# Engine orders planned with a later landing for the loads that queue behind the weights, in an attention and feed-forward kernel

## The chip, the cores and the metric

The kernel runs on one core of one Trainium2 chip. The metric is the device time of one execution in microseconds (us), as the median of several executions. A smaller number is better.

A core has five engines with queues of their own: TensorE (PE) for matmuls, VectorE (DVE), ScalarE (ACT), GpSimd (POOL) and SyncE (SP). Each works through its own instructions strictly in the order in which they were written. DMA transfers are issued from queues of SP and POOL.

## The reference

There are two stages. The first is a gated linear attention over 4 batches, 8 heads, 768 steps and a head size of 48:

```python
f = 1.0 / (1.0 + np.exp(-f_logit))
for t in range(S):
    state = f[:, :, t, :, None] * state + np.einsum('bhd,bhe->bhde', k[:, :, t], v[:, :, t])
    y[:, :, t] = np.einsum('bhd,bhde->bhe', q[:, :, t], state)
```

The second takes y as 3072 tokens of 384 features through a feed-forward network with 1536 hidden features:

```python
gate = np.maximum(x @ w_gate, 0.0)
val = x @ w_val
out = gate * val @ w_out
```

Inputs and output are float32; the kernel computes its matmuls in bfloat16.

## The kernel before, in words

**Tiles.** The 768 steps are cut into six chunks c of 128. Within a chunk the batches are taken in pairs pr (b0 = 0 and 2). A load such as q1.0 is q of chunk 1 and pair 0: 384 KB for two batches. For chunks 0 and 1 (twos) two successive chunks are loaded in another layout, and attention_pair works on a pair; from chunk 2 on it is attention_front and attention.

**One pair in attention_pair.** ACT makes exp and ln of f (L583, L584) into bneg. PE sums along the chunk (cum, L592) and ACT takes exponentials of the sums (expo, L606). POOL or DVE multiply k and q with these (hats, L608). PE transposes the hats, first those of k and then those of q, 8 matmuls each for two heads and two chunks (L635), and DVE copies them to qkT (L643). PE forms the scores (L660), DVE masks them into ptm (L669), PE updates the state (L678) and then makes the output rows in the intra block (L698 and L703), which ACT copies to xT (L715).

**The feed-forward part.** It runs one group of 512 tokens per chunk. ffn_hidden makes the gate and val products (L908, 3 matmuls each), ACT takes the relu (L914), and DVE the product gT (L918). ffn_out multiplies with wo (L951), ACT copies to osb (L961), and SP stores it (L965). Its matmuls carry the lowest priority, and are to fill PE between the attention steps.

**The order.** No order is written by hand. Each operation is added to a Plan with the tiles that it reads and writes, an engine, an assumed duration and a priority. schedule() is a list scheduler: again and again it takes the operation that can start earliest in planned time, and of several that can start at once the one with the lowest priority number. The result is one fixed list for each engine, and the waits on semaphores are derived from it afterwards.

**Planned landings.** The loads in the list first are treated more closely:

```python
first = ("f0.0 k0.0 q0.0 v0.0 f0.1 k0.1 q0.1 v0.1 wg0@f0.1 wv0 wg1@q0.1 wv1 wg2 wv2 f1.0@wv1 k1.0 q1.0 v1.0 wo0@q1.0 wo1 wo2 "
         "f1.1 k1.1 q1.1 v1.1").split()
```

The part behind @ is a gate: f1.0 is issued when wv1 has landed, wo0 when q1.0 has landed. The loads f, k, q, v go through SP, the weights wg, wv, wo through POOL. transfers() plays the packets of these two queues against each other. A load of chunk 0 or 1 has 64 packets, of 19 ns each when alone and 27 ns when the two queues alternate; a part of wo has 32 packets, of 62 ns alone and 80 ns in alternation. They begin 2.4 us after the issue (loads) or 2.2 us after it (wo). When the last packet is through, a fixed tail is added and gives the planned landing, Op.land. settle() plans the whole kernel eight times, with the landings of each round as inputs of the next; only the operations in first keep them. Later loads and all stores use a simpler formula in schedule(), which begins where the last of the planned landings ends (flow_free).

So a planned landing has no effect on a transfer by itself. It decides where, on each engine, the operations that depend on a load stand among the others.

Of the kernel before, what the change touches and what calls it, by code (L numbers as in the profile page):

```python
# [5 lines left out]
AF = mybir.ActivationFunctionType  # L6
ALU = mybir.AluOpType
# [35 lines left out]
class Plan:  # L43
# [10 lines left out]
    def add(self, eng, emit, reads=(), writes=(), occ=0.5, lat=0.2, prio=0, opens=(), after=(), follows=()):  # L54
        op = Op(eng, emit, list(reads), list(writes), occ, lat, prio, opens, after, follows)
        op.idx = len(self.ops)
        self.ops.append(op)
        return op
# [128 lines left out]
    def transfers(self):  # L187

        rings = {e: [op for op in self.order[e] if op.parts] for e in ("SP", "POOL")}
        todo, at = {e: [] for e in rings}, {e: 0 for e in rings}  # L190
        issue = {"SP": 0.0}
        held = {e: [] for e in rings}
        sent, owed, t, last = 0, 0, 0.0, None
        pending = None
        sp = rings["SP"]
        queue = {e: [] for e in rings}
        for op in rings["POOL"]:
            queue["POOL"].append([op, op.parts[0], op.start + op.parts[3]])
        nxt = 0

        def feed():
            nonlocal nxt, pending, owed
            while True:
                if pending is not None:
                    if owed - sent > self.depth:
                        return
                    pending.issued = max(t, issue["SP"])
                    issue["SP"] = pending.issued
                    pending = None
                if nxt == len(sp):  # L210
                    return
                op = sp[nxt]
                begin = max(op.ready, issue["SP"])
                if begin > t + 1e-9 and (queue["SP"] or queue["POOL"]):
                    if begin > t + 0.2:
                        return
                nxt += 1
                owed += op.parts[0]
                queue["SP"].append([op, op.parts[0], begin + (op.parts[3] if len(op.parts) > 3 else self.lag)])
                issue["SP"] = begin + op.occ  # L220
                pending = op

        while True:
            feed()
            heads = {e: queue[e][0] for e in queue if queue[e]}
            if not heads:
                break
            can = {e: h for e, h in heads.items() if h[2] <= t}
            if not can:
                times = [h[2] for h in heads.values()]  # L230
                if nxt < len(sp) and pending is None:
                    times.append(max(sp[nxt].ready, issue["SP"]))
                t = max(t + 0.01, min(times))
                continue
            e = next(iter(can)) if len(can) == 1 else ("POOL" if last == "SP" else "SP")
            h = can[e]
            t += h[0].parts[1 if len(can) == 1 else 2] / 1000.0
            last = e
            h[1] -= 1
            if e == "SP":  # L240
                sent += 1
            if h[1] == 0:
                h[0].land = t + (1.6 if e == "POOL" else 0.65 if t < 14.0 else 1.9)
                queue[e].pop(0)

    def settle(self, banks, rounds, early):
        self.depth, self.lag = 250, 2.4
        for i in range(rounds):
            self.schedule(banks)
            if i < rounds - 1:  # L250
                self.transfers()
                for op in self.ops:
                    if op not in early:
                        op.land = op.issued = None
        return self.order
# [47 lines left out]
def bass_hgrn2_outer__then__ffn_reglu_kernel(  # L303
# [8 lines left out]
    out: bass.AP,  # L312
):
    twos = (0, 1)
    pe_hats = set()
    halves = {0: 6, 1: 6, 2: 6}
    x_way = {(c, pr): "tiled" if c < 5 else "xbar" for c in range(6) for pr in range(2)}
    s_twin = {(c, pr) for c in range(6) for pr in range(2)}
# [8 lines left out]
    C = 128  # L327
# [5 lines left out]
    NP = H // 2  # L333
# [14 lines left out]
    hats = sb("hats", [128, NH, 2, H, 64], BF16)  # L348
    NQ = 8
    qkT = sb("qkT", [128, NQ, 2, NP, C], BF16)  # L350
    NM = 4
    ptm_all = sb("ptm", [128, NM, 2, NP, C], BF16)
    ptm = [ptm_all[:, i] for i in range(NM)]
# [34 lines left out]
    add = pl.add  # L388
    gp, ve, sc, te, sy = nc.gpsimd, nc.vector, nc.scalar, nc.tensor, nc.sync
# [7 lines left out]
    def act_t(n):  # L397
        return dict(occ=max(0.18, 0.06 + n / 1150.0), lat=0.14)
# [4 lines left out]
    def pool_t(n):  # L403
        return dict(occ=0.1 + n * 2.2 / 1000.0, lat=0.12)
# [29 lines left out]
    for t, name, src, sname in ((upto, "upto", tri, "tri"), (below, "below", tris, "tris")):  # L434
        add("DVE", lambda t=t, src=src: ve.tensor_tensor(t[:], src[:], same.ap[:, 0:128], ALU.mult), [same, sname], [name],
            occ=0.25, prio=-19)
    add("DVE", lambda: ve.tensor_copy(pick2[:], same.ap[:, 0:128].rearrange("p (b t) -> p b t", b=2)[:, :, 0]), [same], ["pick2"],
        occ=0.1, prio=-19)
    for i, src, name in ((0, upto, "upto"), (1, below, "below"), (1, upto, "upto")):
        lo = [m for m in range(2) if not (i and (name == "upto") != (m == 1))]  # L440
# [3 lines left out]
            prio=-9, **pool_t(64 * len(lo)))  # L444
# [14 lines left out]
    def dma(op, slot, flow, parts, n=1):  # L459

        if slot not in slots:
            slots[slot] = [nc.alloc_semaphore(f"d_{slot}"), 0]
        slots[slot][1] += 16 * n
        op.sem, op.goal = slots[slot]
        op.flow, op.parts = flow, (n * parts[0], *parts[1:])
# [48 lines left out]
    for item in first:  # L514
        item, _, behind = item.partition("@")
        gate = [done[behind]] if behind else []
        if item[0] == "w":
            op = load_w(item[:2], int(item[2:]), gate)
        else:
            c, b = int(item[1]), int(item[3])  # L520
            b0, b1 = (2 * b, 2 * b + 2) if item[2] == "." else (b, b + 1)
            op = load(item[0], c, b0, b1, gate)
# [12 lines left out]
    def hk_(hi):  # L535
        return [f"hk{hi}_0", f"hk{hi}_1"]

    def hq_(hi):
        return [f"hq{hi}_0", f"hq{hi}_1"]

    def qk_(qi):
        return [f"qkT{qi}_{x}{hh}" for x in range(2) for hh in range(2)]

    def tokens(c, b, x, p, lo=0, hi=128, i=None):
        qi = (c * B + b) % NQ
        if c not in twos:
            return qkT[lo:hi, qi, x, p, :]
        row, two = NQ * 2 * NP * C, b % 2
        at = lo * row + (qi - two) * 2 * NP * C + x * 2 * NP * C + p * 2 * C + two * 64
        if i is not None:  # L550
            return bass.AP(tensor=qkT, offset=at + i * C, ap=[[row, hi - lo], [1, 64]])
        return bass.AP(tensor=qkT, offset=at, ap=[[row, hi - lo], [C, 2], [1, 64]])

    t4 = lambda t: t[:, 0:HD].rearrange("p (n j e) -> p n j e", n=NP, j=2)

# [15 lines left out]
    def attention_pair(c, b0):  # L571
        w0 = c * B + b0
        P = w0 * 10
        pr = b0 // 2
# [4 lines left out]
        bi, e0, q0 = (w0 // 2) % NB, w0 % NE, w0 % NQ  # L579
        his = [(w0 + i) % NH for i in range(2)]  # L580
# [6 lines left out]
        for i in range(2):  # L587
# [7 lines left out]
            hi, prod = his[i], {}  # L595
            for x, n in ((1, "k"), (0, "q")):
                e = "DVE" if (i or x if c == 0 else (c, pr, x, i) in on_dve) else "POOL"
# [23 lines left out]
        for j in range(2):  # L621
            lo = 64 * j
# [2 lines left out]
                tot.ap[lo:lo + 64, 0:2 * NP].rearrange("p (n b) -> p n b", n=NP), AF.Exp, scale=-1.0),  # L625
                [tot, "dec0", "dec1"], [f"dec{ai}_{bt}{j}{hh}" for ai in range(2) for hh in range(2)], prio=P + 10,
                follows=[eq_op], **act_t(8))
        for x in (1, 0):
            tp = Bank("tp")

            def transposes(x=x, tp=tp):
                t16 = tp.ap[:, :].bitcast(BF16)
                for p in range(NP):
                    for i in range(2):
                        mm = te.transpose(t16[:, C * (2 * p + i):C * (2 * p + i + 1)],  # L635
                                          hats[:, his[i], x, 2 * p:2 * p + 2, :].rearrange("p h d -> p (h d)"), ident[:])
                return mm
            chain("transposes", "PE", transposes, ["ident"] + [t for hi in his for t in (hk_(hi) if x else hq_(hi))], [tp],
                  occ=0.5, lat=PE_L, prio=P + 4, opens=[tp])
            dst = bass.AP(tensor=qkT, offset=q0 * 2 * NP * C + x * 2 * NP * C, ap=[[NQ * 2 * NP * C, 128], [1, 2 * NP * C]])  # L640
            e = "ACT" if (x, pr) in act_copies else "DVE"
            add(e, (lambda tp=tp, dst=dst: sc.activation(dst, tp.ap[:, :].bitcast(BF16), AF.Copy)) if e == "ACT"
                else (lambda tp=tp, dst=dst: ve.tensor_copy(dst, tp.ap[:, :].bitcast(BF16))),  # L643
                [tp], [f"qkT{q0 + b}_{x}{hh}" for b in range(2) for hh in range(2)], prio=P + 4,
                occ=0.92 if e == "ACT" else 0.61, lat=0.12)

        vs, ms = [(w0 + i) % NV for i in range(2)], [(w0 + i) % NM for i in range(2)]
# [5 lines left out]
        s = [[Bank("s"), Bank("s")] for _ in range(2)]  # L653
# [9 lines left out]
        for its in ((0,), (1,)) if c == 0 else ((0, 1),):  # L663
            at = [t for i in its for t in s[i]]
            chain("scores", "PE", lambda its=its: scores(its), qk, at, occ=0.22 * len(its) + 0.22, lat=PE_L, prio=P + 5, opens=at)
        for i in range(2):
            mask = mask2[:, i, :, :].rearrange("p m t -> p (m t)").unsqueeze(1).to_broadcast([128, NP, C])
            for j in range(2):
                add("DVE", lambda i=i, j=j, mask=mask: ve.tensor_tensor(  # L669
                    ptm[ms[i]][:, j, :, :], s[i][j].ap[:, :].rearrange("p (n t) -> p n t", n=NP), mask, ALU.mult),  # L670
                    [s[i][j], f"mask2_{i}0", f"mask2_{i}1"], [f"ptm{ms[i]}_{j}{hh}" for hh in range(2)], prio=P + 6, **dve_t(512))
# [429 lines left out]
```

## Time and profile before

| | |
|---|---|
| median of 4 runs | 191.53 us |
| lowest and highest | 191.22 and 192.8 us |
| profiled execution, own time | 192.8 us |
| its span, first to last instruction | 191.0 us |
| granted TensorE clock | 1.0 throughout |
| PE busy | 181.7 us (95%) |
| DVE, ACT, POOL busy | 55%, 57%, 39% |
| DMA queues | SP's 28.19 MB, POOL's 3.54 MB |

Busy shares are averages over the span; the loads are read mostly in its first three quarters. PE is pipelined and the ends of its matmuls are modelled, so 95% doesn't say that PE is at its peak. Lines such as L908 are line numbers of the kernel before.

### The profile page before, as it was taken

What the parts mean: (1) busy time and instruction counts of PE and PEld (TensorE: products, weight loads), DVE (VectorE), ACT (ScalarE), POOL (GpSimd) and SP (SyncE); (2) the same over time, 40 slices, a digit from 0 to 9 for tenths busy, and PEclk for the clock granted to TensorE, in tenths of its full rate; (3) what the DMA queues carried; (4) which work ended last, traced back from release to release, by engine and by line L of the source; (5) the groups of instructions that cost most, each with busy time, mean ns of one, the idle gap of its engine ahead of it and who ended that gap; (6) DMA issues with size and microseconds to landing.
All of it is one profiled execution on the core that took longest, in us unless ns stands there. A gap on an engine that the chain in (4) does not pass through costs nothing.

```text
span 191.0 us, 5040 instructions
## 1 busy us (share of the span) xinstructions
PE 181.7 (95%) x2073; PEld 108.9 (57%) x2092; DVE 105.3 (55%) x191; ACT 108.6 (57%) x244; POOL 75.0 (39%) x109
## 2 busy tenths in 40 slices
PE   7978899979999999999999999999999999999995
PEld 2446684546688456768645564554555555544564
DVE  7699766877346867428586274726428323343300
ACT  3763569813889576585877738566533533334322
POOL 8497007861286737536384562908100000000000
PEclk9999999999999999999999999999999999999999
DMA  5999999996999999999999989999531310011113
GB/s 158 325 264 203 207 285 265 221 214 132 250 207 206 223 153 217 225 218 249 168 222 177 225 166 214 180 232 208 127 69 39 86 41 19 23 45 41 41 51 114
DMA packets 108854, 32.04 MB, mean 168 GB/s; under 512 B 101792, under 2 KB 108832, under 8 KB 108832
## 3 DMA queue, kind: packets, MB, share of 16 engines
q1 hardware_dynamic: 104848, 28.19, 69.4%
q0 software_dynamic: 3984, 3.54, 11.7%
q8 instruction: 16, 0.26, 0.6%
q14 instruction: 6, 0.05, 0.1%
HBM read 25.95 MB, written 4.72 MB: 161 GB/s over the span
## 4 chain that ended last, share of the span: by engine, by line
PE 74%; DMA 13%; SPq 7%; POOL 1%; ACT 1%; issue 1%; DVE 0%
PE ps L908 39%; PE ps L951 23%; DMA q_in<-in_q_dram 9%; SPq L486 7%; DMA wv<-in_moe_w_val_dram 5%; PE ps L838 3%; PE ps L803 2%; PE ps L737 1%; PE ps L886 1%; PE ps L931 1%; POOL hats L608 1%; PE ps L698 1%; ACT relu L914 0%; ACT expo L747 0%; PE ps L740 0%
## 5 line engine op out<-in xcount | busy, mean ns | idle before, releaser
L918 DVE TENSOR_TENSOR gT<-relu,ps 128x512 bf16<-128x512 bf16 (+1 forms) x90 | 51.3, 578 | 62.8 <-PE ps L908 36.6
L914 ACT ACTIVATE relu<-ps 128x512 bf16<-128x512 f32 (+1 forms) x90 | 45.8, 513 | 28.5 <-PE ps L908 27.3
L908 PE MATMUL ps<-xT,wv 128*128 128x512 bf16 (+1 forms) x267 | 61.0, 336 | 0.4 <-issue 0.2
L908 PE MATMUL ps<-xT,wg 128*128 128x512 bf16 (+1 forms) x255 | 58.2, 334 | 1.1 <-issue 0.6
L951 PE MATMUL ps<-wo,gT 128*128 128x384 bf16 x276 | 50.0, 326 | 0.0
L908 PEld LDWEIGHTS ps<-xT,wv 128*128 128x128 bf16 x270 | 25.7, 98 | 19.0
L951 PEld LDWEIGHTS ps<-wo,gT 128*128 128x128 bf16 x276 | 26.0, 98 | 17.8
L908 PEld LDWEIGHTS ps<-xT,wg 128*128 128x128 bf16 x270 | 25.1, 98 | 17.6 <-ACT xT L715 0.3
L961 ACT ACTIVATE osb<-ps 128x384 f32<-128x384 f32 x23 | 11.2, 491 | 27.8 <-PE ps L951 27.8
L759 POOL TENSOR_TENSOR hats<-k_in,expo 128x384 bf16<-128x384 f32 x16 | 15.9, 997 | 22.4 <-ACT expo L747 22.4
L813 DVE TENSOR_TENSOR ptm<-ps,tri 128x512 bf16<-128x512 f32 x32 | 20.2, 681 | 2.4 <-PE ps L803 2.4
L568 POOL TENSOR_TENSOR st<-ssum,dec 128x384 bf16<-128x384 f32 x16 | 13.1, 828 | 18.7 <-DVE ssum L566 18.7
L763 POOL TENSOR_TENSOR hats<-q_in,expo 128x384 bf16<-128x384 f32 x16 | 15.7, 998 | 0.5 <-DMA q_in<-in_q_dram 0.5
L566 DVE TENSOR_TENSOR ssum<-ps,st 128x384 f32<-128x384 f32 x16 | 8.7, 553 | 5.6 <-PE ps L886 5.5
L669 DVE TENSOR_TENSOR ptm<-ps,mask 128x512 bf16<-128x512 f32 x16 | 9.9, 681 | 1.1 <-PE ps L660 1.0
L747 ACT ACTIVATE expo<-ps 128x384 f32<-128x384 f32 x16 | 7.9, 492 | 1.8 <-PE ps L740 1.7
L715 ACT ACTIVATE xT<-ps 128x384 bf16<-128x384 f32 x8 | 4.2, 593 | 7.9 <-PE ps L703 7.9
L749 ACT ACTIVATE expo<-ps 128x384 f32<-128x384 f32 x16 | 8.0, 500 | 0.0
L867 ACT ACTIVATE xT<-ps 128x384 bf16<-128x384 f32 x12 | 5.3, 487 | 4.2 <-PE ps L838 4.2
L793 POOL CAST vpad<-v_in 128x384 bf16<-128x384 f32 x16 | 7.6, 505 | 0.0
L730 ACT ACTIVATE bneg<-f_in 128x768 bf16<-128x768 f32 x8 | 6.8, 846 | 0.1
L728 ACT ACTIVATE f_in<-f_in 128x768 f32<-128x768 f32 x8 | 6.7, 842 | 0.0
(83 smaller groups left out, 159.8 us busy)
## 6 DMA issues: line engine op xcount, KB each, us to landing
f_in<-in_f_logit_dram SPq DMA_DIRECT2D x12, 384.0 KB, 5.8
k_in<-in_k_dram SPq DMA_DIRECT2D x12, 384.0 KB, 5.7
q_in<-in_q_dram SPq DMA_DIRECT2D x12, 384.0 KB, 4.9
v_in<-in_v_dram SPq DMA_DIRECT2D x12, 384.0 KB, 5.4
out_dram<-osb SPq DMA_DIRECT2D x23, 192.0 KB, 2.2
wg<-in_moe_w_gate_dram POOLq DMA_DIRECT2D x3, 384.0 KB, 7.8
wv<-in_moe_w_val_dram POOLq DMA_DIRECT2D x3, 384.0 KB, 8.5
wo<-in_moe_w_out_dram POOLq DMA_DIRECT2D x3, 384.0 KB, 8.3
```

The source lines that it names most:

```text
L486: op = add("SP", lambda: sy.dma_start(dst, src), [], in_keys(n, c, b0, b1), occ=0.45 if both else 0.7 if one else 1.0, lat=0.9, prio=c * 1 ...
L566: add("DVE", lambda: ve.tensor_tensor(tmp[:, :], kv.ap[:, 0:HD], s_old[:, :], ALU.add), [kv, f"S{b}_{(c + 1) % 2}"], [key], prio=P + 8, ** ...
L568: add("POOL", lambda: gp.tensor_tensor(t4(s_new), t4(tmp), rate, ALU.mult), [key] + dk, [f"S{b}_{c % 2}"], prio=P + 8, **pool_t(HD))
L669: add("DVE", lambda i=i, j=j, mask=mask: ve.tensor_tensor(ptm[ms[i]][:, j, :, :], s[i][j].ap[:, :].rearrange("p (n t) -> p n t", n=NP), ma ...
L759: add("POOL", lambda: gp.tensor_tensor(hk, kin[:, b % 2, :, :], ex[:, 1, :].rearrange("p (h d) -> p h d", h=H), ALU.mult), in_keys("k", c, ...
L763: add(e, lambda: engine[e].tensor_tensor(hq, qin[:, b % 2, :, :], ex[:, 0, :].rearrange("p (h d) -> p h d", h=H), ALU.mult), in_keys("q", ...
L813: add("DVE", lambda mi=mi, j=j, s=s: ve.tensor_tensor(ptm[mi][:, j, :, :], s.ap[:, :].rearrange("p (n t) -> p n t", n=NP), mask, ALU.mult) ...
L908: mm = te.matmul(bank.ap[:, 0:n], wt[:, kt, j * 128:(j + 1) * 128], xT[xi][:, kt, n0:n1], start=(kt == 0), stop=(kt == NK - 1))
L914: add("ACT", lambda: sc.activation(relu[ri][:, 0:n], gate.ap[:, 0:n], AF.Relu), [gate], [f"relu{ri}"], prio=P, **act_t(n))
L918: add("DVE", lambda: ve.tensor_tensor(gT[gi][:, j, n0:n1], relu[ri][:, 0:n], val.ap[:, 0:n], ALU.mult), [val, f"relu{ri}"], [f"gT{gi}_{j}_ ...
L951: mm = te.matmul(o[b].ap[:, 0:DM], gT[gi][:, j, b * C:(b + 1) * C], wo[:, j, :], start=(j == 0), stop=(j == NJ - 1))
L961: add("ACT", lambda b=b, oi=oi: sc.activation(osb[oi][:, :], o[b].ap[:, 0:DM], AF.Copy), [o[b]], [f"osb{oi}"], prio=P, **act_t(DM))
```

## The change

The number 1.9 in transfers() becomes an entry of a tuple self.tail, which settle() sets to (1.6, 2.6). The 1.6 for POOL's transfers and the 0.65 for SP's landings ahead of 14 us stay as they were.

```diff
-                h[0].land = t + (1.6 if e == "POOL" else 0.65 if t < 14.0 else 1.9)
+                h[0].land = t + (self.tail[0] if e == "POOL" else 0.65 if t < 14.0 else self.tail[1])
...
-        self.depth, self.lag = 250, 2.4
+        self.depth, self.lag, self.tail = 250, 2.4, (1.6, 2.6)
```

The rest of the diff brings switches, and sets them to what the kernel does already: all pairs of chunks 0 and 1 are in pe_hats, so that their hats are transposed on PE with the strides of before, and by_pool is empty.

```diff
-    pe_hats = set()
+    pe_hats = {(0, 0), (0, 1), (1, 0), (1, 1)}
+    by_pool = set()
...
-        at = lo * row + (qi - two) * 2 * NP * C + x * 2 * NP * C + p * 2 * C + two * 64
+        sx, sp, si = (2 * NP * C, 2 * C, C) if (c, b // 2) in pe_hats else (NP * C, C, 2 * NP * C)
+        at = lo * row + (qi - two) * 2 * NP * C + x * sx + p * sp + two * 64
...
+        for i in range(2) if (c, pr) not in pe_hats else ():
+            op = add("SP", lambda i=i: sy.dma_start(qkT[:, q0 + i, :, :, :].rearrange("p x n t -> p (x n) t"),
+                                                    hats[:, his[i], :, :, :].rearrange("p x h d -> p (x h d)"), transpose=True),
...
-        for x in (1, 0):
+        for x in (1, 0) if (c, pr) in pe_hats else ():
...
+                if (c, pr, i, j) in by_pool:
```

More of the change, by code (lines that the diff above doesn't have):

```diff
@@ L548, in tokens @@
         row, two = NQ * 2 * NP * C, b % 2
-        at = lo * row + (qi - two) * 2 * NP * C + x * 2 * NP * C + p * 2 * C + two * 64
+        sx, sp, si = (2 * NP * C, 2 * C, C) if (c, b // 2) in pe_hats else (NP * C, C, 2 * NP * C)
+        at = lo * row + (qi - two) * 2 * NP * C + x * sx + p * sp + two * 64
         if i is not None:
-            return bass.AP(tensor=qkT, offset=at + i * C, ap=[[row, hi - lo], [1, 64]])
-        return bass.AP(tensor=qkT, offset=at, ap=[[row, hi - lo], [C, 2], [1, 64]])
+            return bass.AP(tensor=qkT, offset=at + i * si, ap=[[row, hi - lo], [1, 64]])
+        return bass.AP(tensor=qkT, offset=at, ap=[[row, hi - lo], [si, 2], [1, 64]])
     t4 = lambda t: t[:, 0:HD].rearrange("p (n j e) -> p n j e", n=NP, j=2)
@@ L627, in attention_pair @@
                 follows=[eq_op], **act_t(8))
-        for x in (1, 0):
+        for i in range(2) if (c, pr) not in pe_hats else ():
+            op = add("SP", lambda i=i: sy.dma_start(qkT[:, q0 + i, :, :, :].rearrange("p x n t -> p (x n) t"),
+                                                    hats[:, his[i], :, :, :].rearrange("p x h d -> p (x h d)"), transpose=True),
+                     hk_(his[i]) + hq_(his[i]), qk_(q0 + i), prio=P + 3, occ=1.3, lat=1.2)
+            dma(op, f"qkT{q0 + i}", 1.4, (64, 20, 28))
+        for x in (1, 0) if (c, pr) in pe_hats else ():
             tp = Bank("tp")
@@ L668, in attention_pair @@
             for j in range(2):
+                if (c, pr, i, j) in by_pool:
+                    keys = [f"ptm{ms[i]}_{j}{hh}" for hh in range(2)]
+                    add("ACT", lambda i=i, j=j: sc.activation(ptm[ms[i]][:, j, :, :], s[i][j].ap[:, :].rearrange("p (n t) -> p n t", n=NP),
+                                                              AF.Copy), [s[i][j]], keys, prio=P + 6, **act_t(512))
+                    add("POOL", lambda i=i, j=j, mask=mask: gp.tensor_tensor(ptm[ms[i]][:, j, :, :], ptm[ms[i]][:, j, :, :], mask, ALU.mult),
+                        keys + [f"mask2_{i}0", f"mask2_{i}1"], keys, prio=P + 6, **pool_t(512))
+                    continue
                 add("DVE", lambda i=i, j=j, mask=mask: ve.tensor_tensor(
```

## Prediction

> **What bounds the kernel now.** I began with the chain that ended last, in order of time, then took PE's waits and PE's timeline around the longest of them. Ahead of 43 us the chain is loads, not arithmetic:
>
> ```profile
> 11.76 0.77 POOL wg L507
> 12.53 8.91 DMA wv<-in_moe_w_val_dram
> 21.45 0.37 SPq L486
> ...
> 29.15 11.47 DMA q_in<-in_q_dram
> 40.62 0.07 issue
> 40.69 1.96 POOL hats L608 x2
> 42.64 0.05 issue
> 42.69 0.62 PE ps L635 x8
> ```
>
> Columns: start, duration, what. The loads of chunk 1 start when wv1 has landed; q of its second pair (I write q1.1, its pair 1.1, the first pair 1.0) is issued at 29.15 and lands 11.47 us later, at 40.62; POOL makes two hats; PE transposes them at 42.69. From there the chain is PE almost without a break: no "issue" piece after 43 us is over 0.2 us. So the end is 42.69 plus the PE work still undone then. A gain has to put more PE work ahead of that point.
>
> PE's waits in the whole run say what can be had:
>
> ```profile
> PE ps L1001 <- DVE zeros L414: 1.3, 1, 1.3
> PE ps L635 <- POOL hats L608: 1.1, 1, 1.1
> PE ps L660 <- DVE qkT L643: 1.1, 2, 0.6
> PE ps L908 <- issue: 0.8, 5, 0.2
> ```
>
> Columns: total us, times, longest. The first is the start, and the two of L660 lie at 10.9 and 17.5 us, ahead of any load behind the weights. The second is the one that late landings cause. PE's timeline around it:
>
> ```profile
> 37.68 0.81 PE L908 MATMUL ps<-xT,wg 128*128 128x512 bf16 x3
> 38.42 0.64 PE L660 MATMUL ps<-qkT 48*64 48x128 bf16 x32
> 38.99 0.62 PE L635 MATMUL ps<-ident,hats 128*128 128x128 bf16 x8
> 39.45 0.81 PE L908 MATMUL ps<-xT,wv 128*128 128x512 bf16 x2
> 40.10 1.46 PE L951 MATMUL ps<-wo,gT 128*128 128x384 bf16 x8
> 42.69 0.62 PE L635 MATMUL ps<-ident,hats 128*128 128x128 bf16 x8 [1.13 <-POOL hats L608]
> 43.24 0.74 PE L698 MATMUL ps<-ptm,vpad 64*32 64x128 bf16 x64
> 43.91 0.35 PE L703 MATMUL ps<-qkT,st 128*32 128x128 bf16 x12
> ```
>
> PE stands 1.13 us in front of the q transposes of pair 1.1, and behind them in its queue stands the intra block of pair 1.0 (L698 and L703, 43.24 to 44.2), whose own inputs were ready: its last mask product ended on DVE at 41.67. The order, not the data, keeps it back.
>
> **What the change does, part by part.** All switches but one are neutral: pe_hats holds exactly the pairs that go through attention_pair, so the transposes stay on PE and the strides stay as they were; by_pool is empty. No instruction, DMA or byte is added or removed. Left is the number 1.9 that becomes 2.6: the tail in transfers() between a load's last packet and its planned landing, for SP landings after 14 us. Only the loads of the list first keep these landings, so it concerns the eight loads of chunk 1. The planned times below are the order's inputs, not times of the chip.
>
> (1) The planned landings. By the code the first transfer begins 2.4 us after its planned issue at 21.49 and each takes 64 x 19 ns = 1.216 us, so with 1.9 the landings are 27.00 (f1.0), 28.22, 29.44 (q1.0), 30.65, 31.87, 33.08 (k1.1). The trace (issue plus time to landing) has 26.5, 28.2, 29.2, 31.1, 32.3, 33.4. With 2.6 each moves 0.70 later: the plan gets worse for the first three, better for the next three by little.
>
> q1.1 moves the other way. wo0 is gated on q1.0, and its packets begin 2.2 us after: at 31.64 before, at 32.34 now. q1.1 has the queue from 31.18. Before, 24 of its 64 packets go alone and 40 alternate with wo at 27 + 80 = 107 ns: 31.64 + 4.28 + 1.9 = 37.82. Now 61 go alone and 3 alternate: 32.66 + 2.6 = 35.3. v1.1 likewise goes from 43.96 to about 42.1. In the trace they land at 40.62 and 43.83. So "later landings" holds for six of eight, and the two late ones are planned still earlier.
>
> [...] The row first: 11.47 us from issue to landing for q1.1, and 5.0 to 6.7 for the six ahead of it. [...] By the row, q1.1 shares the DMA engines with wo0 and wo1 and is 2.8 us behind even the old plan: gain up to 1.13. I take the row.
>
> (2) The order on PE, replanned by hand. With f1.0 0.70 later, the bn of pair 1.0 is planned ready at 29.81 instead of 29.34; PE is free at 29.67, so one FFN block (3 matmuls, 0.65 us) goes ahead of the cum matmuls (L592). Everything of pairs 1.0 and 1.1 that hangs on cum moves about 0.65 to 0.8 us later, and one FFN block earlier: no PE work appears or vanishes. On POOL q1.1's landing isn't what binds in either plan: its two hats follow the k hats, and end at 41.29 instead of 40.64. The scores of pair 1.0 now come before an FFN block, so its intra block is ready at about 40.4. When PE is free at 40.69 the intra block is the earliest, and goes **ahead of** the q transposes; before, the transposes went first.
>
> (3) On the chip. The hats cannot end before q1.1's landing plus the 0.07 and 1.96 of the rows, 42.64, in either order. Before, PE ran out at 41.56. Now it has 0.96 us more (43.24 to 44.20) to do there: 1.13 - 0.96 leaves 0.17 of stall, and 0.96 is gained. Against it: on ACT one relu (0.60 in its row) comes ahead of the four exponentials of pair 1.0, which makes the first hats about 0.2 later than PE gets to them; on DVE one gT (0.69) slips between the two q products of that pair (2.35 for both in their row), for another 0.2 to 0.3. Those lie ahead of 42.69, so part of them comes out of the remaining stall: I charge 0.1, with 0 and 0.5 as the bounds. Net gain 0.85, between 0.4 and 1.0.
>
> (4) What moves past the queues. With v1.1 planned 1.9 earlier, the loads of chunk 2 are planned about 1.9 earlier too (f2.0 at 44.4; the trace has 45.4). On SP the load of v2.0 (48.59 now) then comes ahead of the two stores of out (47.54), which wait for ACT: good for the load, and the stores have nobody behind them. POOL keeps its sequence of weight loads; wo2 (issued 34.97) goes 0.7 later but stands behind wo1, which lands at 40.3: free. The cum matmuls of chunk 2 (50.37 now) come 1 to 2 us forward. Their f has landed at 45.4 and needs 0.83 + 0.84 on ACT, so 47.1; I place PE there at 47.5 or later: 0, with 0.5 as the upper bound.
>
> **The sum.** The profiled execution took 192.8 with a span of 191.0; minus 0.85 that is 191.95 and 190.15. It is the highest of the four runs, so I set the 0.85 against the median: 191.53 - 0.85 = 190.7. For gains of 0.4 to 1.2 (the last, should other waits go too): 190.3 to 191.1.
>
> **Rivals.**
> A. The stall stays or moves: intra isn't sorted ahead (a planned 0.6 us decides that), or the waits of pair 1.0 eat it up. For it: the pair's k hats and transposes are already tight (PE waits 0.15 for vpad at 35.08). Against: the margin of 0.6 is most of an FFN block. Time 191.5.
>
> B. Slower. The chunk 2 fronts are ordered by landings that the chip doesn't deliver: f2.1 would be planned at about 53.2 and landed at 55.2 in the trace. With PE about 0.95 behind its plan, ACT would stand 1.05 us in front of that exp, with the relus of the FFN queued behind it; PE has four banks for gate and val and stops after about two more blocks of 0.33. It decides once such waits add to more than 0.85: two pairs at 1.05 each give 191.53 - 0.85 + 2.1 = 192.8; four would give 194.9. For it: the plan is now optimistic where it was about right. Against: PE takes none of its waits there today, ACT is idle 43% of the span, and the issues of these loads move forward as well.
>
> C. More than the stall: PE's other gaps go too. From 54 us PE is busy 133.36 of 137.00, but its waits there are under 1 us together, and nothing in the change is aimed at them. Time 189.5.
>
> **How the numbers follow.** Forecast (190.3 to 191.1) 0.44; A (within 0.4 of 191.5) 0.22; B 0.30, of which half is over 1%; C 0.04. Over 1% (1.9 us, about what a measurement of this kernel can tell from no change): faster 0.04, slower 0.16, within 0.80. The range leaves out C's far end and the quarter or so of B where more than two pairs wait: 189.8 to 193.4.
>
> **What would show it.** Right: in PE's timeline L698 and L703 of pair 1.0 stand ahead of the L635 x8 that follows q1.1, and its wait on hats is under 0.4; q1.1 still lands near 40.6; one more L908 group before the first L592 behind 29 us; v2.0 issued before the first stores. Wrong: the L635 wait at 1 us or more (A); PE waiting on relu, gT or f_in between 50 and 100 us (B); or q1.1 landing elsewhere, which would undo (3).

## The result, and the profile after

| | before | after |
|---|---|---|
| median | 191.85 us (53 runs) | 193.65 us (32 runs) |
| lowest and highest | 191.22 to 195.59 us | 192.33 to 196.24 us |
| profiled execution, own time | 192.80 us | 193.21 us |
| its span | 191.0 us | 191.5 us |

The ratio is 1.0078, with a 95% interval of 1.0061 to 1.0095: the change costs about 1.5 us. That is under 1%, but clearly a loss, where a gain of 0.85 was forecast. Medians are over all executions and ratios over those within 1.5% of the fastest of their kernel, so the two can differ. Line numbers move: L635 is now L642, L698 and L703 are L712 and L717, L592 is L594, L608 is L610, L908 is L922, L951 is L965.

PE's waits in the profile after (total us, times, longest):

```profile
PE ps L717 <- issue: 0.9, 1, 0.9
PE ps L712 <- issue: 0.8, 1, 0.8
PE ps L642 <- POOL hats L610: 0.5, 1, 0.5
```

The wait of 1.1 us in front of the transposes has become one of 0.5. But in the intra block (L712) there is a new stop of 0.85 (0.8 in this view), put down to "issue", that is, to nothing that the profile can name. The stop at L717 lies at 22.45 us; in the profile of before it is there too, with 0.62:

```profile
22.50 0.24 PE L703 MATMUL ps<-qkT,st 128*32 128x128 bf16 x4 [0.62 <-issue]
```

The chain that ended last has the first two one behind the other (start, duration, what):

```profile
28.92 10.00 DMA q_in<-in_q_dram
...
39.06 1.96 POOL hats L610 x2
41.02 0.05 issue
41.06 0.62 PE ps L642 x8
41.68 0.65 PE ps L965 x4
42.34 0.66 PE ps L712 x61
42.99 0.85 issue
43.84 0.21 PE ps L712
```

q1.1 lands at 38.92, 1.7 us earlier than in the profile shown for before, and still PE waits for two hats after it. Which two, and for which transposes, shows in the timelines of POOL and PE:

```profile
37.40 0.99 POOL L610 TENSOR_TENSOR hats<-k_in,expo 128x384 bf16<-128x384 f32 x1 [0.87 <-ACT expo L608]
39.06 1.00 POOL L610 TENSOR_TENSOR hats<-q_in,expo 128x384 bf16<-128x384 f32 x1 [0.67 <-DMA q_in<-in_q_dram]
40.01 1.00 POOL L610 TENSOR_TENSOR hats<-k_in,expo 128x384 bf16<-128x384 f32 x1
40.96 1.00 POOL L610 TENSOR_TENSOR hats<-q_in,expo 128x384 bf16<-128x384 f32 x1
```

```profile
39.74 0.81 PE L965 MATMUL ps<-wo,gT 128*128 128x384 bf16 x4
41.06 0.62 PE L642 MATMUL ps<-ident,hats 128*128 128x128 bf16 x8 [0.51 <-POOL hats L610]
41.52 0.81 PE L965 MATMUL ps<-wo,gT 128*128 128x384 bf16 x4
42.26 0.73 PE L712 MATMUL ps<-ptm,vpad 64*32 64x128 bf16 x63
43.84 0.21 PE L712 MATMUL ps<-ptm,vpad 64*32 64x128 bf16 x1 [0.85 <-issue]
43.98 0.35 PE L717 MATMUL ps<-qkT,st 128*32 128x128 bf16 x12
44.27 0.62 PE L642 MATMUL ps<-ident,hats 128*128 128x128 bf16 x8
```

The order on POOL is now k, q, k, q: a q hat, which waits for q1.1, stands **ahead of the second k hat**. In before it was k, k, q, q:

```profile
36.64 1.96 POOL L608 TENSOR_TENSOR hats<-k_in,expo 128x384 bf16<-128x384 f32 x2 [0.86 <-ACT expo L606]
40.69 1.95 POOL L608 TENSOR_TENSOR hats<-q_in,expo 128x384 bf16<-128x384 f32 x2 [1.30 <-DMA q_in<-in_q_dram]
```

So the wait of 0.51 is in front of the *k* transposes of pair 1.1. The intra block does go ahead of the q transposes (44.27), as forecast, but it comes behind the k transposes, which now depend on q1.1 as well.

**Where the time goes.** For this the profile of before that was shown is a bad partner, as the next section shows; a second one has a span of 189.9, 1.6 less than after. By the end of the last gate or val block PE is at 40.30 in it and at 39.74 after; before has 0.46 of k transposes behind it by then, so after is 0.1 ahead. In the two chains the scores of pair 1.1 begin at 43.91 and 46.19: 2.28 apart. After has four more wo matmuls (0.65) done by then, which leaves a loss of 1.63, or 1.73 with the 0.1 that it was ahead. Of this 1.36 are the two stops, 0.51 and 0.85; the rest is not taken apart. 1.63 is the whole difference of the spans: in this pair of profiles nothing is lost or won behind 46 us.

### The profile page after: what moved, and what is told of

Read it like the earlier page. It is cut to its first block, busy times and chain, and to the rows that moved or that the text cites. A ratio compares the mean times of both kernels' runs of the same rounds, so it can differ in the third digit from the quotient of the medians.

```text
span 191.5 us, 5041 instructions
## 1 busy us (share of the span) xinstructions
PE 181.1 (95%) x2075; PEld 108.9 (57%) x2092; DVE 104.9 (55%) x191; ACT 109.1 (57%) x244; POOL 75.1 (39%) x109
## 4 chain that ended last, share of the span: by engine, by line
PE 76%; DMA 12%; SPq 7%; issue 2%; POOL 1%; ACT 0%; POOLq 0%
PE ps L922 41%; PE ps L965 23%; DMA q_in<-in_q_dram 8%; SPq L487 7%; DMA wv<-in_moe_w_val_dram 5%; PE ps L852 3%; PE ps L817 2%; PE ps L751 1%; PE ps L900 1%; PE ps L945 1%; POOL hats L610 1%; PE ps L712 1%; PE ps L642 1%; PE ps L754 0%; PE ps L864 0%
## 5 line engine op out<-in xcount | busy, mean ns | idle before, releaser
L922 PE MATMUL ps<-xT,wv 128*128 128x512 bf16 (+1 forms) x264 | 60.2, 335 | 0.4 <-issue 0.2
L922 PE MATMUL ps<-xT,wg 128*128 128x512 bf16 (+1 forms) x260 | 59.5, 335 | 0.9 <-issue 0.3
L965 PE MATMUL ps<-wo,gT 128*128 128x384 bf16 x276 | 49.0, 326 | 0.1
L965 PEld LDWEIGHTS ps<-wo,gT 128*128 128x128 bf16 x276 | 26.5, 98 | 18.2
L922 PEld LDWEIGHTS ps<-xT,wg 128*128 128x128 bf16 x270 | 25.3, 98 | 18.3 <-ACT xT L729 0.3
L922 PEld LDWEIGHTS ps<-xT,wv 128*128 128x128 bf16 x270 | 25.1, 98 | 18.4
```

What stands on the lines that cost most here:

```text
L922: mm = te.matmul(bank.ap[:, 0:n], wt[:, kt, j * 128:(j + 1) * 128], xT[xi][:, kt, n0:n1], start=(kt == 0), stop=(kt == NK - 1))
L965: mm = te.matmul(o[b].ap[:, 0:DM], gT[gi][:, j, b * C:(b + 1) * C], wo[:, j, :], start=(j == 0), stop=(j == NJ - 1))
```

## The experiments

The explanations under test were the late k hat on POOL; the stop in the intra block; and, as a third, something further back, which the earlier plan for v1.1 brings with it. Kernels that were measured together share their runs of before.

### One landing, one order

**The kernel before again, unchanged.**

> The kernel before once more, for a second profile. Theory 1 (the profiled execution of before, 192.8 us, was a late one): q of chunk 1 pair 1 lands earlier than 40.62 us, nearer to 39, PE waits clearly less than 1.13 us in front of the q transposes of that pair, and the span is near 190. Rival (the 1.13 us are typical of before): landing 40.3 to 40.9, wait 1.0 to 1.3, span 190.8 to 191.2.

Ratio 0.9998 (0.9963 to 1.0033). Its profiled execution took 191.68 us, and the wait that the prediction started from isn't in it. POOL, then PE:

```profile
39.54 1.94 POOL L608 TENSOR_TENSOR hats<-q_in,expo 128x384 bf16<-128x384 f32 x2
```

```profile
40.30 1.46 PE L951 MATMUL ps<-wo,gT 128*128 128x384 bf16 x8
41.59 0.61 PE L635 MATMUL ps<-ident,hats 128*128 128x128 bf16 x8
42.13 0.74 PE L698 MATMUL ps<-ptm,vpad 64*32 64x128 bf16 x64
```

q1.1 landed at 39.31, not 40.62, and the q transposes follow the output blocks with no bracket. The two profiled executions of before are 192.80 - 191.68 = 1.12 us apart, and the stall was 1.13: the stall is what made the first one long.

**POOL's order back to k, k, q, q; all planned landings as in the change.** For pair 1.1 the q hats get a priority number higher by one:

```diff
-  prio=P + 3 - x + i,
+  prio=P + 3 - x + i + (1 if not x and (c, pr) == (1, 1) else 0),
```

> The changed kernel, with the priority number of the q hats of chunk 1 pair 1 raised by one, so that POOL makes the two k hats ahead of the two q hats again (k, k, q, q instead of k, q, k, q). Theory 1 (the early planned landing of q1.1 put a q hat, which waits for the late load, ahead of the second k hat, and PE's k transposes wait for it): the 0.51 us wait in front of the k transposes goes, and the time falls by 0.4 to 0.8 us against the change, to a ratio of about 1.004. Rival (the loss lies in the stop of 0.85 us inside the intra block): the stop stays, or grows by what was saved, and the ratio stays 1.006 to 1.010.

193.45 us, 1.0052 (1.0026 to 1.0078). q1.1 landed late, at 41.28, and yet the k transposes (40.38) have no wait: the order does what it was meant to. The loss does not vanish with it. The stop at 22 us was 1.48 in this profile, one of 0.26 stood in the intra block, and wv1 landed at 22.89 where the two profiles of before have 21.43 and 21.66, so the profile is of a late execution.

**The kernel before with one landing moved.** The tail stays 1.9, and only q1.1 is planned at 35.26, as the change has it:

```diff
+    fixed = {'q3_0': 35.26}
...
+                    elif op.writes[0] in self.fixed:
+                        op.land = self.fixed[op.writes[0]]
```

> The kernel before with a single planned landing altered: q1.1 at 35.26 instead of 37.82 us, the value that it has under the change; all other landings keep the tail of 1.9. POOL's order becomes k, q, k, q for that pair, PE makes the k transposes one feed-forward block later, and intra of pair 0 stays behind the q transposes. Theory 1 (this landing alone carries the loss): ratio 1.005 to 1.010, PE waits for the second k hat. Rival (the shift of the six other landings carries it): ratio 0.998 to 1.002.

193.36 us, 1.0069 (1.0041 to 1.0097): nearly the whole loss of 1.0078 comes with **this one landing**. POOL's order becomes k, q, k, q. Its own profile shows the wait elsewhere: PE stood 1.02 us, until 36.00, for DVE's q hats of pair 1.0 and came to the k transposes only at 41.13, when the hats were there. So the time agrees with the explanation, and this profile neither shows nor contradicts it.

**The change without its two early landings.** The same edit on after, with {'q3_0': 37.82, 'v3_0': 43.96}, the values of before; the six 0.70 later landings stay.

> The changed kernel with the planned landings of q1.1 and v1.1 put back to 37.82 and 43.96 us, those of before; the other six stay 0.70 later. Intra of pair 0 still goes ahead of the q transposes, POOL makes k, k, q, q. Theory 1 (the two early landings carry the loss): ratio 0.997 to 1.002. Rival (the intra block placed ahead of the q transposes carries it, with its stop of 0.85 us): ratio 1.004 to 1.008 and the stop still there.

193.21 us, 1.0041 (1.0015 to 1.0066), in two groups: three runs from 191.17 to 191.44, the others at 192.81 and more. The profiled one is of the early group (191.31) and has no stop in the intra block. So something else is left in most of its executions.

### The stop in the intra block

The stop always precedes the same two matmuls of the program: numbers 347 and 599 in PE's sequence of matmuls, 252 apart. PE has some 4,165 matmuls and weight loads, about one load to each matmul, and the profile lists a queue that carries something in 16 packets:

```profile
q8 instruction: 16, 0.26, 0.5%
```

These are 16 KB each. If all of them are PE's, which the profile doesn't say, the 4,165 instructions give an estimated 63 bytes an instruction and 260 instructions to a packet. With a load to each matmul, 252 matmuls are then about two packets. Between 10 and 50 us the profiles here hold 21 stops of at least 0.2 us that are put down to issue. By the DMA records of the traces, the packets in question took 0.88 to 0.98 us, and the stop ended 1.2 to 1.6 us after the packet had ended (in after 41.38 to 42.26, and 43.84; in before at 22 us, 20.15 to 21.05, and 22.50), which is 2.2 to 2.5 us after it had begun. The stop then goes with how soon PE gets from the packet's start to matmul 599. In after it was there 1.6 us later and stood 0.85; with k, k, q, q it was there 2.2 us later and stood 0.26; in the two profiles of before it was there 4.5 and 3.3 us later and did not stand.

The author's reading is that PE waits there for its next block of instructions. It was tested by moving the two matmuls to later places in the sequence: each warming matmul at the start is cut into four, which puts about 54 matmuls ahead of everything else.

```diff
-  return te.matmul(spare[:, 0:WARM], zeros[:, 0:128], zeros[:, 0:WARM], ...)
+  for at in range(0, WARM, 128):
+      mm = te.matmul(spare[:, at:at + 128], zeros[:, 0:128], zeros[:, at:at + 128], ...)
+  return mm
```

> The changed kernel with each of the 17 or so warming matmuls at the start (512 columns of zeros) cut into four of 128 columns: the same columns and about the same time, but some 50 more matmuls, so that every later PE instruction sits some 100 places further in PE's instruction stream. The order of all real work is untouched. Theory 2 (the stops called issue inside intra blocks, 0.92 us at 22.45 and 0.85 us at 43.84 in the change, are PE waiting for its next 16 KB of instructions): both stops move or go, PE's waits on issue fall under 0.5 us, and the time falls by 0.8 to 1.7 us, to a ratio of 0.999 to 1.004. Rival (the stops come from the data, or from whatever the block reads): the stops stay at the same two blocks and the ratio stays near 1.008.

> The kernel before with the same cut of the warming matmuls. Theory 2: its stop at 22.5 us (0.62 and 0.91 in two profiles) goes, and the time falls by 0.4 to 0.9 us, ratio 0.995 to 0.998. Rival: the stop stays, ratio 0.999 to 1.001.

In the profiles the stops at 22 us and in the intra block of pair 1.0 were gone from both kernels, as the reading wants. In after a short one came up elsewhere, in front of matmul 221 of the longer sequence; that is 126 ahead of 347, or about one packet by the estimate:

```profile
14.56 0.24 PE L712 MATMUL ps<-ptm,vpad 64*32 64x128 bf16 x5 [0.26 <-issue]
```

Against what was expected, the times got no better: 195.43 us, 1.0174 (1.013 to 1.0218) for after, 193.1 us, 1.0039 (1.0013 to 1.0065) for before. In after PE waited 1.17 for the k hat (q1.1 landed at 40.60) and 1.31 for DVE's q hats of pair 1.0; in before 1.02 for the latter. Why the gain at 22 us doesn't show in the times is not shown; the loads of chunk 1, at least, were issued no earlier (from 22.17 and 21.60 us on, against 21.31 in after and 21.45 in before).

**After again, and after without its two early landings again**, one execution of each.

> The changed kernel once more, for a second profile. Both theories: span 191 to 192.5. Theory 1: PE waits again in front of the k transposes of pair 1.1, by 0.4 us or more, because a q hat stands ahead of the second k hat. Theory 2: a stop of 0.7 us or more again inside the intra block at about 43 us. If neither is there at such a span, both fall.

> A second profile of the changed kernel with q1.1 and v1.1 planned as before. Its 20 times lie in two groups, three at 191.2 to 191.4 and the rest from 192.8; the first profile is of the early group (191.31). Theory 2: a profile of the later group shows a stop on issue of 0.8 us or more inside an intra block, at 22 or at 42 us. Rival: it shows wv1, and with it all loads of chunk 1, landing 1 us or more later than 21.06, and no longer stop.

After took 194.41 us with both stops on PE: 0.23 for the k hat (q1.1 at 39.87, PE late itself) and 1.11 in the intra block. In the other (198.68 us) PE stood 5.0 us for vpad and the granted clock was 0.983, so its time says nothing; a stop of 1.48 in front of matmul 599 was there.

### The stop removed by cut matmuls

In the feed-forward group 0 the 36 gate and val matmuls of 256 columns (b0 = 2) are issued as two of 128 columns. That puts 36 matmuls ahead of the intra block at the cost of 36 more instructions. The two halves are accumulated alternately in one bank, and these gate and val products aren't the reference's.

```diff
+  step = 128 if (c, b0) == (0, 2) else n
   for kt in range(NK):
-      mm = te.matmul(bank.ap[:, 0:n], ..., xT[xi][:, kt, n0:n1], ...)
+      for at in range(0, n, step):
+          mm = te.matmul(bank.ap[:, at:at + step], ..., xT[xi][:, kt, n0 + at:n0 + at + step], ...)
```

> The kernel before with the same cut of 36 matmuls, as the control: before has no stop in its intra block of pair 1.0. Theory 2: ratio 0.999 to 1.002. Rival (the cut itself costs or saves time): outside of that.

> The changed kernel, with the 36 gate and val matmuls of 256 columns that group 0 makes for its second two batches (at 24 to 27 us) each cut into two of 128 columns: same work and nearly the same PE time, 36 matmuls more. That leaves the stop at 22 us where it is and moves every later position in PE's stream by 72 instructions. Theory 2 (the stop of 0.85 to 1.11 us in the intra block of pair 1.0 is PE waiting for its next 16 KB of instructions, because k transposes and intra come too close behind each other): the stop in that block goes, the wait of 0.2 to 0.5 us for the k hats stays, ratio 1.001 to 1.005. Rival (the stop belongs to the block or its data): it stays at the first part of intra, ratio 1.007 to 1.010.

> The changed kernel with POOL's order k, k, q, q for pair 1.1 and the same cut of 36 matmuls; both early planned landings stay. Theory 1 with theory 2: ratio 0.996 to 1.000. Rival (the early landing of v1.1, which moves the loads of chunk 2 and its state step forward, costs time by itself): ratio 1.003 or more.

> The changed kernel with q1.1 and v1.1 planned at 37.82 and 43.96 as before, and the same cut of 36 matmuls. Theory 2 with theory 1 (late k hat and intra stop together are the whole loss): neither is left, the times gather at 191.2 to 191.6 and the ratio is 0.995 to 0.999, with PE reaching the scores of pair 1.1 ahead of before. Rival (something else of the six later landings costs time): ratio 1.003 or more.

| kernel, with the cut | us | ratio to before | k hat wait | stop in intra |
|---|---|---|---|---|
| before | 192.01 | 1.0004 (0.9981 to 1.0027) | none | none |
| after | 194.24 | 1.0110 (1.0046 to 1.0174) | 1.04 | none |
| after, k, k, q, q | 193.07 | 1.0011 (0.9980 to 1.0042) | none | none |
| after, two landings of before | 191.73 | 0.9988 (0.9966 to 1.0010) | none | none |

The cut by itself costs nothing that shows (first row; the stop at 22 us, ahead of the cut, stays in all four). It removes the stop in all of the changed kernels, yet only those in which the k hats come first are back at the time of before. PE's timeline of the last one, with L646 the transposes, L972 the output blocks, L716 and L721 the intra block:

```profile
40.38 0.61 PE L646 MATMUL ps<-ident,hats 128*128 128x128 bf16 x8
40.82 1.46 PE L972 MATMUL ps<-wo,gT 128*128 128x384 bf16 x8
42.22 0.73 PE L716 MATMUL ps<-ptm,vpad 64*32 64x128 bf16 x64
42.88 0.35 PE L721 MATMUL ps<-qkT,st 128*32 128x128 bf16 x12
43.16 0.62 PE L646 MATMUL ps<-ident,hats 128*128 128x128 bf16 x8
```

Not a bracket in it, although q1.1 landed at 40.22. This is the order that the prediction had in mind, intra ahead of the q transposes and no wait, and its time is that of before: there was nothing to win.

### The cut without loss, and other ways

Now each half is accumulated on its own (the loop over `at` outside, the one over `kt` inside), and the products are the reference's. One kernel removes the stop with no added matmul: after with k, k, q, q on POOL and the intra block of pair 1.0 held back in the plan, so that it comes behind the q transposes.

```diff
-        chain("intra", "PE", rows, ...)
+        late = chain("intra", "PE", rows, ...)
+        late.floor = 41.5 if (c, pr) == (1, 0) else 0.0
```

The last kernel is before with only v1.1 planned early, at 42.11.

> The changed kernel with the 36 matmuls of group 0 cut in two, each half accumulated on its own. Theory 2: no stop in the intra block of pair 1.0. Theory 1: the wait for the second k hat stays and is the larger the later q1.1 lands (0.5 at 38.9, 1.0 at 39.5), so the ratio lies at 1.004 to 1.008. Rival (with the stop gone the whole loss is gone): 0.998 to 1.002.

> The changed kernel with q1.1 and v1.1 planned as before and the 36 matmuls cut in two, each half accumulated on its own. Theories 1 and 2 together: no stop, no wait for hats, ratio 0.997 to 1.001. If the 1.13 us wait of the profiled before were typical of before, this kernel, which has the intra block in that place, would reach 0.995 or less.

> The changed kernel with POOL's order k, k, q, q for pair 1.1 and the intra block of pair 1.0 held back until after the q transposes and one more output block; no matmul added. Theory 2 (the stop depends on how fast PE gets from the k transposes to the middle of intra): with 0.65 and 0.45 us more work between them the stop goes, ratio about 1.001 to 1.003. Rival: the stop stays in the block, ratio 1.005.

> The kernel before with one planned landing altered: v1.1 at 42.11 instead of 43.96 us. POOL keeps k, k, q, q and intra of pair 0 stays behind the q transposes; the state step of pair 1.1 and the loads of chunk 2 are ordered earlier. Theory 3 (the early v1.1 costs time of its own, by waits of PE around 100 to 112 us): ratio 1.002 to 1.005, such waits in the profile. Rival (it costs nothing): 0.999 to 1.001.

After with the cut: 194.93 us, 1.0074 (1.0041 to 1.0108), no stop, 0.67 of waiting for the k hat. With the two old landings and the cut: 192.6 us, 1.0005 (0.9969 to 1.0042), neither. With intra late: 192.78 us, 1.0021 (0.9992 to 1.0051), no stop, and a wait in front of the q transposes, as the first profile of before had it:

```profile
42.50 0.62 PE L642 MATMUL ps<-ident,hats 128*128 128x128 bf16 x8 [0.56 <-POOL hats L610]
```

With v1.1 early: 193.28 us, 1.0029 (0.9997 to 1.006), which could be nothing or most of the loss; its profile again had a wait of 1.02 for DVE's q hats, and none of those that were expected at 100 to 112 us.

At the end after and after with the cut were measured side by side on one chip.

> The changed kernel, on the same chip and in the same rounds as the cut version. Ratio to before 1.006 to 1.0095 as recorded; the profile shows the wait for the k hats, and the stop in the intra block of 0.8 us or more.

> The changed kernel with the 36 matmuls of group 0 cut in two, beside the changed kernel itself. If the stop in the intra block is worth time while the k hat is still late, its ratio lies 0.003 to 0.005 under that of the changed kernel of this call; if the late hat alone sets the time, the two ratios agree within 0.002.

193.52 us, 1.0050 (1.0026 to 1.0074), and 194.38 us, 1.0096 (1.0062 to 1.0131). With the stop taken away, after got no faster. It even measured slower, which neither of the two expectations has. The profiles say why nothing was gained; first POOL and PE of after:

```profile
40.41 0.99 POOL L610 TENSOR_TENSOR hats<-q_in,expo 128x384 bf16<-128x384 f32 x1 [1.46 <-DMA q_in<-in_q_dram]
41.36 0.99 POOL L610 TENSOR_TENSOR hats<-k_in,expo 128x384 bf16<-128x384 f32 x1
```

```profile
42.41 0.62 PE L642 MATMUL ps<-ident,hats 128*128 128x128 bf16 x8 [1.29 <-POOL hats L610]
43.61 0.73 PE L712 MATMUL ps<-ptm,vpad 64*32 64x128 bf16 x63
44.54 0.21 PE L712 MATMUL ps<-ptm,vpad 64*32 64x128 bf16 x1 [0.21 <-issue]
```

And PE of the one with the cut:

```profile
43.01 0.62 PE L642 MATMUL ps<-ident,hats 128*128 128x128 bf16 x8 [1.78 <-POOL hats L610]
44.21 0.73 PE L712 MATMUL ps<-ptm,vpad 64*32 64x128 bf16 x64
```

q1.1 landed at 40.27 and 40.88. POOL stands idle for it with the second k hat behind it in its queue; that hat ends 2.1 us after the landing, and PE stands in front of the k transposes until then. The longer this wait, the shorter the stop: in the three profiles of after they are 0.51 and 0.85, 0.23 and 1.11, 1.29 and 0.21, together 1.36, 1.34 and 1.50. Who removes one of them keeps the other.

### The whole picture

| | stop in the intra block left | stop removed |
|---|---|---|
| q hat ahead of the second k hat | after 1.0078 and 1.0050 | 1.0110, 1.0074, 1.0096 |
| k hats first | 1.0052, 1.0041 | 1.0011, 0.9988, 1.0005, 1.0021 |

("Left" means that the sequence of matmuls was not changed; how long the stop is varies from one execution to the next. Left out are the two kernels with cut warming matmuls, whose waits for DVE's q hats at 35 to 36 us disturb the comparison, and those built on before.) Only the lower right corner has intervals that all hold 1. The numbers are from several chips, and single intervals overlap; it is the pattern over eleven entries that carries, together with the brackets in the profiles. With every execution counted, the means are 1.007 to 1.008 upper left, 1.010 to 1.013 upper right, about 1.005 lower left and 0.998 to 1.004 lower right: the same order, with less between the two lower corners. No version was faster than before.

## Why the prediction was wrong

**Step (1), the planned landings: right, and misread.** q1.1 is planned at about 35.3, as worked out. The long way of this load was there again: 10.0 us from issue to landing after, where before had 11.47. But "planned still earlier" was then costed by what it does on PE alone. Before, this landing was planned 2.8 us ahead of where the trace had it (37.82 against 40.62). The change makes that 5.4, and an order that is built on it puts other work behind it.

**Step (2) failed, in one sentence:** "On POOL q1.1's landing isn't what binds in either plan: its two hats follow the k hats". With q1.1 planned at 35.3, a q hat and the second k hat are both ready when POOL is free; their priority numbers are equal, and the scheduler took the q hat. On the chip the q hat isn't ready, and the k hat waits behind it for DMA data that it does not need (POOL stood 0.67 us in after, and 1.46 in its third profile). The order on PE was replanned by hand and came out as forecast; the order on POOL was asserted.

**Step (3) had two wrong terms.** "The hats cannot end before q1.1's landing plus the 0.07 and 1.96" holds in every profile. But what waits for the second of them had changed: after, it is the k transposes. Before, when those hats end, PE has the k transposes and two output blocks done. After, it has one output block done: 0.45 + 0.65 = 1.1 us more are still to do at the same moment. In place of a rest of 0.17 plus 0.1 the wait measured 0.23 to 1.78 over the seven profiles of changed kernels with this order on POOL. The other term is the 1.13 itself. It was the stall of one late execution (192.80, said to be the highest of four, and used all the same); of three profiles of before's order, the other two have q1.1 at 39.31 and 39.45 and no wait. Where the median has no stall there is nothing to gain, and the kernels free of both stops measure 0.9988 to 1.0021, not the 0.9956 of the forecast.

**What wasn't in the prediction:** the stop of 0.85 in the intra block. A stop of the same kind, 0.62 at 22.50, stood in the profile that the prediction worked from, and was passed over. In the two profiles of before the instruction packet of that place came at 39.19 and 39.27, some 3 to 4 us ahead of the block; in after it came at 41.38, within 1 us of it. By moving the intra block up behind the k transposes, the forecast order itself took away the work that had stood between. The stop's worth is the difference of the lower row of the table, about 0.4 to 0.5%, once the k hats come first; with a late k hat none shows.

**Step (4) held.** v2.0 is issued ahead of the stores (44.26, and the stores at 48.51), the cum matmuls of chunk 2 come to 49.10 without a wait (50.37 and 49.27 in the two profiles of before), and one more gate or val block stands ahead of the first L594 (31.02, where the L592 of before has 30.43).

**The rivals.** B had the right sign, but in the profile of after it isn't B's mechanism that shows: ACT doesn't wait for f2.1, nor PE on chunk 2, and the loss is complete by 46 us. In other executions a part of B is there. Behind 60 us PE stands 0.16 to 1.1 us in six of the eleven profiles of kernels that plan v1.1 early, and in none of the nine others. The longest such wait is in after with the first cut:

```profile
111.86 0.34 PE L900 MATMUL ps<-vpad,hats 128*128 128x96 bf16 x4 [1.03 <-POOL vpad L807]
```

Of A the heading came true, a stall that moves, but by neither of the two ways that it names; C didn't happen. The rival that decided, a wait on another engine's queue that moves with the same landing, was not listed. The median after is 193.65, 0.25 above the range.

**Open:** how much v1.1's earlier plan adds. The waits behind 60 us speak for a part of its own, the times don't settle it: 1.0029 with an interval that reaches below 1, and with the stop removed and the k hats first, 1.0011 and 1.0021 for the kernels that have it, 0.9988 and 1.0005 for those that don't. Open too: what sets the moment at which an instruction packet starts; why the loads start 1 to 2 us later in some executions (wv1 landed between 21.0 and 23.1); and why after with the cut measured above after side by side, beyond its later landing in the one profile.

## What to carry to other kernels

When a planned time moves, replan every queue that reads it, not only the bottleneck's: an instruction that is moved ahead of another on an idle engine hands its own wait to all that stands behind it. In the third profile of after POOL's 1.46 us for q1.1 left PE standing 1.29 for a k hat. A change of one constant need not move everything one way; here a gate turned "later" into "earlier" for the one load that mattered. And take the stall that is to be removed from several executions: the profiled one may be the only one that has it.

## What the runs showed of the hardware

**PE stood in front of the same two matmuls.** Stops of up to 1.48 us stood in front of matmuls 347 and 599, in stretches of many small ones (L712, L717). Both left their places when 54 matmuls were put ahead of them, the second also with 36. All 21 stops ended 2.2 to 2.5 us after an instruction packet had started. That a late block of instructions is the cause is the author's reading of the packets and of the shifted kernels; no record names it.

**DVE's two products took 3.78 us where they started ahead of POOL's, and 2.35 where they started behind.** In the second profile of before POOL starts its k hats 0.33 us ahead of DVE's q hats, in before with cut warming matmuls 0.17 us behind them. DVE and POOL of the former, then of the latter:

```profile
32.06 2.35 DVE L608 TENSOR_TENSOR hats<-q_in,expo 128x384 bf16<-128x384 f32 x2 [0.49 <-ACT expo L606]
31.73 2.27 POOL L608 TENSOR_TENSOR hats<-k_in,expo 128x384 bf16<-128x384 f32 x2 [0.65 <-ACT expo L606]
```

```profile
30.85 3.78 DVE L608 TENSOR_TENSOR hats<-q_in,expo 128x384 bf16<-128x384 f32 x2 [0.49 <-ACT expo L606]
31.02 1.97 POOL L608 TENSOR_TENSOR hats<-k_in,expo 128x384 bf16<-128x384 f32 x2
```

Between these two DVE loses 1.43 us where it starts first, and POOL gains 0.30. All four profiles in which PE waits 1.02 to 1.31 us for DVE's q hats, at 35 to 36 us, are of this kind: POOL was still issuing weights when the exponentials were ready. In three of them the two products stand together on DVE and took 3.78 to 4.05 us; in the fourth, with a gT between them, 3.01 and 0.55. In fifteen of the other sixteen POOL starts first, and there is no such wait: DVE took 2.35 there, or 1.07 to 1.08 and 0.75 to 0.76 with a gT between, and POOL 2.27, against 1.96 to 1.97 in the four. The sixteenth has neither pair by 36 us. What makes DVE's products longer is not shown.
